# The load of v for batches 4 to 7 is requested behind the first gate block of the next group

## The chip, the cores and the metric

The kernel runs on one core of one Trainium2 chip. The metric is the device time of one execution in microseconds (us), the median of the runs. The engines are named as in the profile: PE (matrix products; PEld is its weight load), DVE, ACT, POOL, and SP, which only issues transfers. POOL issues all loads of q, k and v, so its instruction order also sets the order of these transfers.

## The reference

The computation has two parts, one after the other. The first is attention with a sliding window and a decay per head, for 8 batches of 8 heads, 576 rows and 64 columns. The second is a feed-forward block on the 4608 x 512 result.

```python
scores = scale * np.matmul(q, k.transpose(0, 1, 3, 2))      # 8 batches, 8 heads, 576 x 576
mask = (rel >= 0) & (rel < 128)
scores = np.where(mask, scores + bias[None], -1e9)
attn = softmax(scores)
x = np.matmul(attn, v)                                       # then reshaped to (4608, 512)
g, val = x @ w_gate, x @ w_val                               # (512, 1536) each
out = (gelu(g) * val) @ w_out                                # (1536, 512)
```

## The kernel before

All order is written by hand: each engine executes its instructions in the order of the program, and nothing is moved by a scheduler.

The feed-forward block goes over 9 groups of 512 tokens (`g` = 0 to 8), attention over 8 batches of 576 rows. They are interleaved: while group `g` is in its feed-forward block, the batch `b = g + 2` is in its scores and the batch `b - 1 = g + 1` in its values. A group has two stretches.

* **The gate stretch**, twelve blocks `f` = 0 to 11 of 128 hidden columns. For blocks 0 to 5 and 10 and 11, `gate_val` (L659) makes the products with `w_gate` and `w_val`; ACT takes gelu of the one (L666) and DVE multiplies it with the other into `hT` (L667). Blocks 6 to 9 go together through `gate_quad` (L842), which needs seven products on sums of x instead of eight. POOL makes these sums (`combine_x`, L800), and POOL multiplies the upper halves of the quad's hidden values (L889).
* **The output stretch**, `out_products` (L762): the product with `w_out`, also seven products instead of eight, called `P(1)` to `P(7)`, each for two halves `a` = 0 and 1. They need sums of hidden blocks, `combine_left` (L737); POOL makes those of blocks 0 to 5, DVE those of blocks 6 to 11 at f = 11, behind POOL's L889. Between the products stand the scores of batch g + 2 (`scores2`, L307; exponentials on ACT, L236; masks on DVE, L241) and the values of batch g + 1 (`values`, L508), which read `vb`. Results leave PSUM through `gather_out` (L909 to L924); where a product adds on to a PSUM bank (`P(4)` after `P(7)`, say), the bank has to be read first, for `P(4, 0)` by DVE's L919.

Transfers. POOL requests q, k and v of a batch with five DMA instructions each (`load`, L117: four of 128 rows and one of 64). q and k go to the tiles `qs` and `ks`; SP turns them into `qT` and `kT` with transposing transfers at the start of the next group (`transposes_dma`, L180 and L187), behind the landing of q and k. v goes straight to `vb[b % 2]`, where the values read it, one group and a half after the request. The tile `vb[g % 2]` also holds the gelu values of group g's quad.

Three places on POOL matter here. At f = 3, a copy of two elements of block 3 into the tile `mark` (L1336) makes POOL wait until DVE has written block 3; behind it stand `combine_x` and four `combine_left`. (In group 2 the same place is f = 0.) At f = 5 two more `combine_left` stand. At f = 6 stands the quad with L889, and right behind it the requests: q and k of batch g + 3, then v of batch g + 2.

Of the kernel before, what the change touches and what calls it, by code (L numbers as in the profile page):

```python
# [36 lines left out]
def kernel(  # L37
# [10 lines left out]
    nc = tc.nc  # L48
    B, H, S, D = q.shape
# [49 lines left out]
    mark = consts.tile([1, 2], BF16, name="mark")  # L99
# [13 lines left out]
    def load(t, src, b, js=range(5), last=0):  # L113
        for j in js:
            n = rows(j)
            at = last if j == 4 else 0
            nc.gpsimd.dma_start(  # L117
                out=t[at:at + n, j, :].rearrange("p (h d) -> p h d", h=H),
                in_=src[b][:, 128 * j:128 * j + n, :].rearrange("h p d -> p h d"))
# [5 lines left out]
    def load_v(b, js=range(5)):  # L125
        load(vb[b % 2], v, b, js, 64)
# [44 lines left out]
    def transpose(b, what, c, copy):  # L171
        ps = bank().bitcast(BF16)
        for n, lo in ((0, 0), (1, 384)):
            transpose_runs(b, n, what, c, ps[:, lo:576])
        for n, lo in ((0, 0), (1, 384)):
            untangle(copy, b, n, what, c, c + 1, ps[:, lo:576])

    def transposes_dma(b):
        def of_k():
            nc.sync.dma_start_transpose(  # L180
                out=kT[b % 2].rearrange("p c (j t) -> p (c j) t", t=128),
                in_=ks[b % 2].rearrange("p j x -> p (j x)"))

        if b > 4:
            of_k()
        for j in range(5):
            nc.sync.dma_start_transpose(  # L187
                out=qT[b % 2][:, :, 128 * j:128 * j + 128], in_=qs[b % 2][:, j, :])
        if b <= 4:
            of_k()  # L190
# [193 lines left out]
    def add(b, c0, copy=None, what=(0, 2, 1)):  # L384
        hs = slice(2 * c0, 2 * c0 + 4)
        P = Ps[b % 2].rearrange("p h (n y) -> p h n y", y=64)[:, hs]
        to = T.rearrange("p h (n y) -> p h n y", y=64)[:, hs]
        if 0 in what:
            for x in (0, 1):
                half = slice(64 * x, 64 * x + 64)  # L390
                nc.vector.tensor_tensor(
                    out=to[half, :, x:x + 7:2], in0=P[half, :, 0:10:3], in1=P[half, :, 1:11:3],
                    op=ALU.add)
        if 2 in what:
            nc.vector.tensor_copy(out=to[0:64, :, 8], in_=P[0:64, :, 12])
            nc.vector.tensor_tensor(
                out=to[64:128, :, 8], in0=P[64:128, :, 11], in1=P[64:128, :, 12], op=ALU.add)
        if 1 in what:
            for x in (0, 1):
                half, n = slice(64 * x, 64 * x + 64), 4 - x  # L400
                (copy or nc.vector.tensor_copy)(
                    out=to[half, :, x + 1:x + 2 * n:2], in_=P[half, :, 2:3 * n:3])
# [237 lines left out]
    hid = {}  # L640
# [43 lines left out]
    def store():  # L684
        for args in stores:
            nc.sync.dma_start(**args)
        stores.clear()
# [41 lines left out]
    def combine_left(g, lo, hi, which=(0, 1, 2, 3), engine=nc.vector):  # L729
        x, ns = halves(g), slice(lo, hi)  # L730
        a11, a12, a21, a22 = (x[:, ns, e, h, :] for h in (0, 1) for e in (0, 1))
        s1, s2, s4 = (left[:, n, ns, :] for n in range(3))
        steps = ((s1, a21, a22, ALU.add), (s2, s1, a11, ALU.subtract),
                 (s4, a12, s2, ALU.subtract), (a21, a11, a21, ALU.subtract))
        for n in which:
            to, a, b, op = steps[n]
            engine.tensor_tensor(out=to, in0=a, in1=b, op=op)  # L737
# [215 lines left out]
    for h in (0, 2, 4, 6):  # L953
        for w, src in ((0, q), (1, k)):
            (nc.scalar if w and h == 0 else nc.sync).dma_start(
                out=raw[w][h // 4].rearrange("p (h x) -> p h x", h=4)[:, h % 4:h % 4 + 2, :],
                in_=src[0][h:h + 2, 0:384, :].rearrange("h (p r) d -> p h (r d)", r=3))
# [114 lines left out]
    for do in inverse_a:  # L1072
        do[1]()
    dve(out=pairs1.rearrange("p x (h d) -> p h x d", d=64),
        in_=vb[1].rearrange("p j x -> p (j x)")[:, 0:1536].rearrange(
            "p (h x d) -> p h x d", h=H, x=3))
# [46 lines left out]
    for n in range(4):  # L1123
        nc.gpsimd.dma_start(
            out=wo[:, 3 * n:3 * n + 3, :],
            in_=moe_w_out[384 * n:384 * n + 384, :].rearrange("(c p) f -> p c f", p=128))
# [155 lines left out]
    for g in range(NG):  # L1282
        if 1 <= g < B - 2:
            transposes_dma(3 if g == 1 else g + 2)
        if g >= B - 1:
            for f in range(NF):
                if f in QUADS:
                    gate_quad(g, f)
                elif not any(f0 < f < f0 + 4 for f0 in QUADS):
                    gate_val(g, f)  # L1290
                if f == 4:
                    store()
                if f == 5:
                    combine_left(g, 0, 2, (0, 1), engine=nc.gpsimd)
                if f == 6:
                    combine_left(g, 2, 3, (0, 1))
                    combine_left(g, 0, 2, (3, 2), engine=nc.gpsimd)
            for which in ((0, 1), (3,), (2,)):
                for lo, hi in ((3, 5), (5, 6)) if 0 in which else ((2, 5), (5, 6)):
                    combine_left(g, lo, hi, which)  # L1300
            out_products(g)
            continue
        if g == 1:
            room = rooms(1)
            sums = combine_weights(6, nc.vector)
            for do in sums[:5]:
                do()
        for f in range(9 if g == 0 else 0, NF):
            if f == 6 and g:
                gate_quad(g, 6, room if g == 1 else None,  # L1310
                          (lambda: gather(g + 1)) if g in (2, B - 2) else None)
            elif not (g and 6 < f < 10):
                gate_val(g, f)
            if g == 1:
                for do in {0: sums[5:7], 1: sums[7:]}.get(f, ()):
                    do()
                if f in (1, 2, 3):
                    combine_x(1, 0, 256, {1: (0,), 2: (1, 2), 3: (3,)}[f])
                if f in (4, 5, 10, 11):
                    combine_right({4: 0, 5: 1, 10: 2, 11: 3}[f])  # L1320
            if f in put_off:
                put_off.pop(f)()
            if f == 1:
                store()
            if g == 0 and f == 10:
                masks_of_last_blocks(0, 8)
            if g == 0 and f == 9:
                for c in range(4):
                    for w in (0, 1):
                        transpose(1, w, c, (act, dve)[w])  # L1330
            if g < 2:
                continue
            if g == 2 and f == 2:
                add(3, 2, act, (1,))
            if f == (0 if g == 2 else 3):
                nc.gpsimd.tensor_copy(out=mark, in_=hid[g][0:1, f, 510:512])  # L1336
                combine_x(g, engine=nc.gpsimd)
            if f == 3 and 2 < g < B - 2:
                combine_left(g, 0, 2, (0, 1, 3, 2), engine=nc.gpsimd)
            if f == (5 if g == 2 else 4):  # L1340
                sums4(g + 1)
            if f == 5:
                if 2 < g < B - 2:
                    combine_left(g, 2, 3, (0, 1), engine=nc.gpsimd)
                    gather(g + 1)
                else:
                    combine_left(g, 0, 3, (0, 1), engine=nc.gpsimd)
            if g == B - 2 and f == 2:
                combine_x(g + 1, 0, 192)
            if f == (11 if g == 2 else 6):  # L1350
                spread_dma(g + 1)
            if f == 6:
                if g + 3 < B:
                    load_qk(g + 3)
                if g + 2 < B:
                    load_v(g + 2)
            if f == 11:
                combine_left(g, 3, 6, (0, 1))
        if g == 1:
            nc.gpsimd.tensor_copy(out=mark, in_=kT[1][0:1, 0, 512:514])  # L1360
            load_qk(4)
            load_v(3)
        if g == 0:
            nc.gpsimd.memset(Ps[0][:, :, 0:64], 0.0)
            for t in (qs[1], ks[1]):
                nc.gpsimd.memset(t[64:128, 4, :], 0.0)
        if g in PRODUCTS:
            out_products(g)
        else:
            for item in steps(g):  # L1370
                if isinstance(item, int):
                    out_part(g, item)
                else:
                    RUN[item[0]](*item[1:])
            store()
        if g == 0:
            load_v(2)
            nc.gpsimd.tensor_copy(out=mark, in_=qT[0][0:1, 0, 512:514])
            load_qk(3)
# [30 lines left out]
```

## Time and profile before

| | |
|---|---|
| runs | 328.99, 327.66, 327.49 us (median 327.66) |
| the profiled execution | 328.3 us, span in the profile 326.5 us |
| busy share of the span | PE 97%, DVE 79%, ACT 67%, POOL 60% |
| granted PE clock | full in all 40 slices |
| groups 3, 4 and 5, from block 0 to the next group's block 0 | 33.77, 33.77 and 33.78 us |

Times in rows are us from the start of the span. A row of the timeline gives start, length, engine, line, operation, tiles and shapes, the number of instructions that were merged, and in brackets how long the engine had been idle and what ended the wait. The length of a merged row runs from its first start to its last end. A row of the windows gives the length of the stretch, then the busy us of each engine with the number of its instructions in parentheses, the granted clock, the DMA share and GB/s.

### The profile page before, as it was taken

Reading aid. Unit: us, or ns where it says so; the run is one execution under the profiler, and the core shown is the slowest. Engines: PE = TensorE matmul, PEld = TensorE weight load, DVE = VectorE, ACT = ScalarE, POOL = GpSimd, SP = SyncE. Lnnn points to the kernel's source line nnn. Section 1 sums busy time; section 2 is a strip of 40 time slices with the busy share of each in tenths; the row PEclk is TensorE's granted clock in tenths of the full one; section 3 lists DMA queues with packets and bytes.
Section 4 is the critical chain, followed back from the end, with each engine's and each line's share of the span. In section 5 each row is a group of like instructions: output and inputs, shape, how many; then the busy total and the mean of one; then the engine's idle time right before and its main releaser. Section 6 shows DMA issues by size and latency. Waiting matters only on the chain.

```text
span 326.5 us, 9488 instructions
## 1 busy us (share of the span) xinstructions
PE 317.4 (97%) x3784; PEld 215.8 (66%) x3784; DVE 256.8 (79%) x506; ACT 219.0 (67%) x417; POOL 195.6 (60%) x224
## 2 busy tenths in 40 slices
PE   8999998999999998999999999999999999999995
PEld 6566645575554767566856685578657787788764
DVE  7889766778779987868798679867996786876692
ACT  8974687567798675857875787578767246636641
POOL 6974689194079897189936994595029475410450
PEclk9999999999999999999999999999999999999999
DMA  8999999999999979976996499949200530003003
GB/s 215 168 196 191 202 173 178 128 160 177 131 175 165 171 147 201 155 137 159 186 190 121 137 182 181 134 126 203 89 15 22 130 130 2 0 2 130 3 0 129
DMA packets 149920, 43.57 MB, mean 133 GB/s; under 512 B 133588, under 2 KB 142964, under 8 KB 149876
## 3 DMA queue, kind: packets, MB, share of 16 engines
q0 software_dynamic: 107456, 18.10, 73.8%
q1 hardware_dynamic: 39104, 18.55, 27.0%
q10 hardware_dynamic: 3316, 6.32, 8.4%
q8 instruction: 29, 0.48, 0.6%
q14 instruction: 15, 0.12, 0.1%
HBM read 43.65 MB, written 9.53 MB: 163 GB/s over the span
## 4 chain that ended last, share of the span: by engine, by line
PE 89%; ACT 3%; DVE 3%; issue 2%; DMA 1%; SPq 0%; ACTq 0%; DVEq 0%
PE ps L659 36%; PE ps L842 18%; PE ps L762 18%; PE ps L508 5%; PE ps L696 4%; ACT P L236 2%; PE ps L307 2%; PE ps L716 2%; PE ps L221 1%; DMA qs<-in_q_dram 1%; PE ps L444 1%; DVE ks L800 1%; PE ps L159 1%; ACT osb L917 1%; DVE xT L547 0%
## 5 line engine op out<-in xcount | busy, mean ns | idle before, releaser
L659 PE MATMUL ps<-xT,wg 128*128 128x512 bf16 (+4 forms) x312 | 71.8, 352 | 0.0
L659 PE MATMUL ps<-xT,wv 128*128 128x512 bf16 (+4 forms) x312 | 71.7, 352 | 0.0
L666 ACT ACTIVATE gelu<-ps 128x512 bf16<-128x512 f32 (+3 forms) x77 | 41.6, 546 | 35.0 <-PE ps L659 31.8
L667 DVE TENSOR_TENSOR hT<-ps,gelu 128x512 bf16<-128x512 f32 (+3 forms) x77 | 46.6, 622 | 19.6 <-PE ps L659 9.4
L236 ACT ACTIVATE P<-ps 128x512 bf16<-128x512 f32 (+1 forms) x108 | 52.3, 577 | 4.1 <-PE ps L307 2.5
L659 PEld LDWEIGHTS <-wv 128*128 128x128 bf16 x312 | 29.5, 98 | 29.7 <-DVE xT L567 0.2
L659 PEld LDWEIGHTS <-wg 128*128 128x128 bf16 x312 | 28.7, 98 | 26.0 <-issue 0.3
L117 POOL DMA_DIRECT2D vb<-in_v_dram x40 | 34.1, 888 | 7.9 <-DMA ks<-in_k_dram 5.9
L241 DVE TENSOR_TENSOR P<-P,emask 128x768 bf16<-128x768 bf16 x60 | 32.0, 553 | 7.3 <-ACT P L236 5.5
L762 PEld LDWEIGHTS <-hT 128*128 128x128 bf16 x336 | 31.9, 97 | 7.6 <-issue 1.0
L887 POOL TENSOR_TENSOR hT<-qT,qs 128x512 bf16<-128x512 f32 x10 | 11.5, 1166 | 30.1 <-ACT qs L853 30.1
L842 PEld LDWEIGHTS <-kept 128*128 128x128 bf16 x256 | 25.0, 98 | 2.9
L762 PEld LDWEIGHTS <-left 128*128 128x128 bf16 x252 | 24.1, 98 | 4.0 <-DVE left L737 0.8
L117 POOL DMA_DIRECT2D ks<-in_k_dram x30 | 25.4, 889 | 1.9 <-DMA qs<-in_q_dram 1.9
L117 POOL DMA_DIRECT2D qs<-in_q_dram x30 | 25.4, 863 | 1.6 <-DMA wo<-in_moe_w_out_dram 0.8
L1336 POOL COPY mark<-hT 1x2 bf16<-1x2 bf16 x5 | 0.9, 174 | 41.3 <-DVE hT L667 41.2
L762 PE MATMUL ps<-right,hT 128*128 128x256 bf16 x168 | 22.2, 272 | 0.6 <-DVE osb L919 0.4
L762 PE MATMUL ps<-right,left 128*128 128x256 bf16 x168 | 20.6, 273 | 0.5 <-DVE left L737 0.5
L762 PE MATMUL ps<-wo,hT 128*128 128x256 bf16 x168 | 21.0, 273 | 0.0
L508 PE MATMUL ps<-P,vb 64*64 64x192 bf16 (+2 forms) x752 | 18.4, 221 | 1.8 <-issue 1.0
L850 DVE TENSOR_TENSOR P<-ps,P 128x512 f32<-128x512 f32 x24 | 15.0, 682 | 6.3 <-PE ps L842 4.3
L850 DVE TENSOR_TENSOR qT<-ps,qT 128x512 f32<-128x512 f32 x20 | 12.9, 686 | 8.9 <-PE ps L842 7.5
(170 smaller groups left out, 624.4 us busy)
## 6 DMA issues: line engine op xcount, KB each, us to landing
out_dram<-osb SPq DMA_DIRECT2D x34, 256.0 KB
rb<-rd ACTq DMA_DIRECT2D x10, 576.0 KB
vb<-in_v_dram POOLq DMA_DIRECT2D x32, 128.0 KB, 6.5
qs<-in_q_dram POOLq DMA_DIRECT2D x24, 128.0 KB, 5.9
ks<-in_k_dram POOLq DMA_DIRECT2D x24, 128.0 KB, 7.7
wo<-in_moe_w_out_dram POOLq DMA_DIRECT2D x4, 384.0 KB, 12.0
wg<-in_moe_w_gate_dram POOLq DMA_DIRECT2D x5, 256.0 KB, 7.2
wv<-in_moe_w_val_dram POOLq DMA_DIRECT2D x5, 256.0 KB, 9.0
```

The source lines that it names most:

```text
L117: nc.gpsimd.dma_start(out=t[at:at + n, j, :].rearrange("p (h d) -> p h d", h=H), in_=src[b][:, 128 * j:128 * j + n, :].rearrange("h p d -> ...
L236: nc.scalar.activation(out=dst, in_=src, func=AF.Exp, scale=0.125)
L241: nc.vector.tensor_tensor(out=dst, in0=dst, in1=m, op=ALU.mult)
L508: mm = nc.tensor.matmul(out=out, lhsT=lhsT, rhs=prob(b)[half, c, i, col:col + q1 - q0], start=all(t[2] != u for t in todo[:n]), stop=True, ...
L659: nc.tensor.matmul(out=ps[:, a:e], lhsT=w[:, c, 128 * f:128 * (f + 1)], rhs=xT[:, c, t0 + lo + a:t0 + lo + e], start=begins and a == 0, st ...
L666: nc.scalar.activation(out=gl[:, 0:n], in_=pg, func=AF.Gelu)
L667: nc.vector.tensor_tensor(out=hid[g][:, f, lo:hi], in0=pv, in1=gl[:, 0:n], op=ALU.mult)
L696: nc.tensor.matmul(out=acc[g], lhsT=hid[g][:, f, 128 * t:128 * (t + 1)], rhs=wo[:, f, :], start=(f == 0), stop=(f == NF - 1))
L762: nc.tensor.matmul(out=made[g, a, into], lhsT=lhsT, rhs=rhs, start=first and i == 0, stop=i == NF // 2 - 1, skip_group_check=True)
L842: nc.tensor.matmul(out=ps[:, 256 * e:256 * e + 256], lhsT=w[:, c, at:at + 128], rhs=x[:, c, :], start=n in (1, 2, 5) and e == 0 and c == 0 ...
L850: nc.vector.tensor_tensor(out=to[u], in0=cut(banks[n, u], to[u].shape[1]), in1=to[u], op=ALU.add)
L887: nc.gpsimd.tensor_tensor(out=out, in0=P5[u], in1=high, op=ALU.mult)
```

## The change

The five requests for v of batch g + 2 behind the quad of group g (g = 2 to 5, batches 4 to 7) are taken out. In groups 3 to 6, behind the gate block f = 0, POOL now copies two elements of that block into `mark`, so that it waits for DVE's write of block 0, and then issues the five requests for v of batch g + 1, which is the batch whose values are made at the end of the same group. The batches 0 to 3, all loads of q and k, and everything on the other engines stay.

```diff
@@ -1332,6 +1332,9 @@
                 continue
             if g == 2 and f == 2:
                 add(3, 2, act, (1,))
+            if g > 2 and f == 0 and g + 1 < B:
+                nc.gpsimd.tensor_copy(out=mark, in_=hid[g][0:1, f, 510:512])
+                load_v(g + 1)
             if f == (0 if g == 2 else 3):
                 nc.gpsimd.tensor_copy(out=mark, in_=hid[g][0:1, f, 510:512])
                 combine_x(g, engine=nc.gpsimd)
@@ -1352,8 +1355,6 @@
             if f == 6:
                 if g + 3 < B:
                     load_qk(g + 3)
-                if g + 2 < B:
-                    load_v(g + 2)
             if f == 11:
                 combine_left(g, 3, 6, (0, 1))
```

The program's instruction order on POOL, between the quad of group 3 and block 3 of group 4 (the name ks_97 is the second k tile, vb_104 the second v tile, here of batch 5; DMASW is a transfer semaphore of POOL's queue):

```order
 L117 DMA ks_97<-in_k_dram 64x8x64 [waits DMASW2_49]
-L117 DMA vb_104<-in_v_dram 128x8x64 [waits DMASW3_49,DVE_49]
-L117 DMA vb_104<-in_v_dram 128x8x64 [waits DMASW4_49,DVE_49]
+L1336 COPY mark<-hT 1x2 [waits DVE_49]
+L117 DMA vb_104<-in_v_dram 128x8x64 [waits DMASW3_49]
+L117 DMA vb_104<-in_v_dram 128x8x64 [waits DMASW4_49]
 L117 DMA vb_104<-in_v_dram 128x8x64 [waits DMASW5_49,Pool_49]
 L117 DMA vb_104<-in_v_dram 128x8x64 [waits DMASW6_49,Pool_49]
 L117 DMA vb_104<-in_v_dram 64x8x64 [waits DMASW7_49]
-L1336 COPY mark<-hT 1x2 [waits DVE_49]
+L1339 COPY mark<-hT 1x2 [waits DVE_49,Pool_49]
 L800 TENSOR_TENSOR left<-xT 128x512 [waits PE_49]
```

Here the new copy stands ahead of the five requests, which so wait for block 0 of group 4; the copy that waits for block 3 (now L1339) and `combine_x` stand directly behind them, as before. One instruction per group is added.

The same engine between the quad of group 5 and block 3 of group 6 (batch 7, for which no q and k follow):

```order
 L889 TENSOR_TENSOR hT<-P_106,vb_104 128x2x256 [waits Activation_49] x2
-L117 DMA vb_104<-in_v_dram 128x8x64 [waits DMASW7_49,DVE_49]
-L117 DMA vb_104<-in_v_dram 128x8x64 [waits DMASW0_49,DVE_49]
+L1336 COPY mark<-hT 1x2 [waits DVE_49]
+L117 DMA vb_104<-in_v_dram 128x8x64 [waits DMASW7_49]
+L117 DMA vb_104<-in_v_dram 128x8x64 [waits DMASW0_49]
 L117 DMA vb_104<-in_v_dram 128x8x64 [waits DMASW1_49,Pool_49]
 L117 DMA vb_104<-in_v_dram 128x8x64 [waits DMASW2_49,Pool_49]
 L117 DMA vb_104<-in_v_dram 64x8x64 [waits DMASW3_49]
-L1336 COPY mark<-hT 1x2 [waits DVE_49]
+L1339 COPY mark<-hT 1x2 [waits DVE_49,Pool_49]
 L800 TENSOR_TENSOR left<-xT 128x512 [waits PE_49]
```

Again only the wait in front of the five requests is new. The rows of PE, DVE, ACT and SP are the same in both programs but for the line numbers of the launch.

## The prediction

> **What bounds the kernel now.** I read the page's chain of work that ended last first (its shares by engine), then windows by group.
>
> ```profile
> PE 89%; ACT 3%; DVE 3%; issue 2%; DMA 1%; SPq 0%; ACTq 0%; DVEq 0%
> 96.38:131.92 35.54, 34.10 (x413) 23.22 (x414) 31.43 (x60) 25.40 (x47) 30.25 (x33) 1.00 1.73 169
> 131.92:165.69 33.77, 33.60 (x413) 23.08 (x412) 26.65 (x54) 24.50 (x43) 25.94 (x29) 1.00 1.37 163
> 165.69:199.46 33.77, 33.60 (x413) 23.08 (x412) 27.70 (x58) 24.51 (x43) 25.25 (x29) 1.00 1.32 160
> 199.46:233.24 33.78, 33.60 (x414) 23.11 (x412) 27.70 (x58) 24.52 (x43) 16.92 (x19) 1.00 1.07 141
> 233.24:265.36 32.12, 31.60 (x323) 21.40 (x322) 26.55 (x54) 17.57 (x30) 17.47 (x17) 1.00 0.25 72
> ```
>
> The windows are groups 2 to 6, the only ones that the change reaches; the first number after the length is PE's busy time. PE sets the end: in groups 3 to 5 it is busy for 33.60 of some 33.77 us. All its idle time in the five groups is 1.44 + 0.17 + 0.17 + 0.18 + 0.52 = 2.48 us. That is all that better transfers could win. No transfer of v stands in the chain. So the question is whether POOL, delayed, makes PE wait.
>
> **The change part by part.** What is taken away first, in group 4, the model for group 5 (the same schedule 33.77 us later):
>
> ```profile
> 161.43 4.27 POOL L117 DMA_DIRECT2D vb<-in_v_dram  x5
> 173.97 0.17 POOL L1336 COPY mark<-hT 1x2 bf16<-1x2 bf16 x1 [8.28 <-DVE hT L667]
> 184.63 2.27 POOL L889 TENSOR_TENSOR hT<-P,vb 128x512 bf16<-128x512 f32 x2
> ```
>
> The five requests are the last things POOL did before it sat idle for 8.28 us until block 3. Their removal frees 4.27 us that nobody waits for: worth 0.
>
> What is put in: the wait for block 0, the small copy, and the same five requests. Block 0's product is the first of the two that DVE makes here:
>
> ```profile
> 169.29 1.29 DVE L667 TENSOR_TENSOR hT<-ps,gelu 128x512 bf16<-128x512 f32 x2
> 172.46 1.45 DVE L667 TENSOR_TENSOR hT<-ps,gelu 128x512 bf16<-128x512 f32 x2
> 186.44 0.69 DVE L667 TENSOR_TENSOR hT<-ps,gelu 128x512 bf16<-128x512 f32 x1 [0.22 <-PE ps L659]
> 187.24 0.56 DVE L737 TENSOR_TENSOR left<-hT 128x768 bf16<-128x768 bf16 x1
> 187.83 0.56 DVE L737 TENSOR_TENSOR left<-left,hT 128x768 bf16<-128x768 bf16 x1
> 190.66 0.42 DVE L919 TENSOR_TENSOR osb<-ps,osb 128x256 f32<-128x256 f32 x1
> 189.00:191.00 2.00, 2.00 (x20) 1.77 (x19) 2.00 (x6) 2.00 (x6) 2.00 (x3) 1.00 1.67 186
> ```
>
> One such product takes 0.69, so block 0 is written at 169.29 + 0.69 = 169.98. I take 0.06 from a DVE write to the copy behind it (an estimate: the second row's products end with block 3 at 172.46 + 1.45 = 173.91, the copy starts at 173.97). Copy at 170.04 to 170.21, five requests to 174.48. The copy for block 3 started at 173.97, so POOL is now late by **0.51 us**. Whether time passes between such a copy and the request behind it, two places show differently (both fives stand directly behind one):
>
> ```profile
> 66.25 4.19 POOL L117 DMA_DIRECT2D qs<-in_q_dram  x5
> 91.90 4.27 POOL L117 DMA_DIRECT2D qs<-in_q_dram  x5 [0.36 <-issue]
> ```
>
> No idle time at the first, 0.36 at the second. I take none, since the requests of the change wait for transfers that were issued over 8 us earlier, and keep 0.51 + 0.36 = 0.87 as the upper bound.
>
> Where does the delay go? From block 3 to L889, POOL has no more than short gaps, so L889 ends not at 186.90 but at 187.41 (bound 187.77). `combine_x` has room:
>
> ```profile
> 175.34 1.15 POOL L800 TENSOR_TENSOR left<-xT,left 128x512 bf16<-128x512 bf16 x1
> 178.35 2.78 PE L842 MATMUL ps<-left,kept 128*128 128x256 bf16 x24
> ```
>
> Its second sum is done at 176.49 and the first product on sums (24 matmuls on `left`) begins at 178.35, 1.9 us later; a later POOL by more than that would stop PE there. But DVE's first L737 reads what L889 writes. It started at 187.24, directly behind DVE's own last product (186.44 + 0.69 = 187.13); now it can start at 187.41 + 0.06 = 187.47. **DVE is late by 0.23 us** (bound 0.59); 0.28 of POOL's delay is free. DVE has no gap up to L919 (2.00 of 2.00 us busy), so L919 moves by as much. And PE waits there: `P(4, 0)` adds to the bank that L919 reads.
>
> ```profile
> 188.38 1.48 PE L762 MATMUL ps<-right,left 128*128 128x256 bf16 x12
> 191.13 0.81 PE L762 MATMUL ps<-right,hT 128*128 128x256 bf16 x6
> 118.63 0.56 DVE L737 TENSOR_TENSOR left<-left,hT 128x768 bf16<-128x768 bf16 x1
> 119.17 1.48 PE L762 MATMUL ps<-right,left 128*128 128x256 bf16 x12
> 121.97 0.42 DVE L919 TENSOR_TENSOR osb<-ps,osb 128x256 f32<-128x256 f32 x1
> 122.44 0.81 PE L762 MATMUL ps<-right,hT 128*128 128x256 bf16 x6 [0.20 <-DVE osb L919]
> ```
>
> L919 ends at 191.08, `P(4, 0)` starts at 191.13. Group 2 shows what a longer DVE does at the same place: from the second L737 to L919 it takes 3.34 us instead of 2.83, and PE takes 3.27 from `P(6, 0)` to `P(4, 0)` instead of 2.75. 0.51 on DVE cost 0.52 on PE: one to one. So group 4 costs 0.23 (at most 0.59), group 5 the same.
>
> Groups 3 and 6 have more room:
>
> ```profile
> 134.38 0.69 DVE L667 TENSOR_TENSOR hT<-ps,gelu 128x512 bf16<-128x512 f32 x1
> 140.20 0.17 POOL L1336 COPY mark<-hT 1x2 bf16<-1x2 bf16 x1 [6.98 <-DVE hT L667]
> 236.84 1.29 DVE L667 TENSOR_TENSOR hT<-ps,gelu 128x512 bf16<-128x512 f32 x2
> 242.56 0.17 POOL L1336 COPY mark<-hT 1x2 bf16<-1x2 bf16 x1 [17.68 <-DVE hT L667]
> ```
>
> With 0.06 + 0.17 + 4.27 = 4.50 behind block 0, the run of requests ends at 135.07 + 4.50 = 139.57 in group 3 and 237.53 + 4.50 = 242.03 in group 6; both are 0.5 to 0.6 before the copy for block 3. They cost 0; without that cover, each 0.1 that the run lasts longer delays POOL by 0.1.
>
> The transfers themselves: v now moves while SP's transposes do.
>
> ```profile
> 170.84 7.21 SPq L187 DMA_TRANSPOSE qT<-qs  x5
> 72.53 8.67 SPq L187 DMA_TRANSPOSE qT<-qs  x5
> 187.58 0.87 PE L307 MATMUL ps<-qT,kT 64*64 64x64 bf16 x44
> vb<-in_v_dram POOLq DMA_DIRECT2D x32, 128.0 KB, 6.5
> 196.08 0.67 PE L508 MATMUL ps<-P,vb 64*64 64x192 bf16 x26
> ```
>
> Beside loads of q and k, at 72.53, the five transposes took 8.67 instead of 7.21 us. 1.5 us more puts the last issue at 179.6 instead of 178.1, and PE reads them at 187.58: hidden by some 8 us; a delay beyond that would reach PE one to one. v lands 6.5 us after its request, near 181, and is read at 196.08: 15 us to spare.
>
> One more thing may stretch the run of requests: DVE's small copies in the same stretch (L395, put off to block 1).
>
> ```profile
> 98.35 0.48 DVE L395 COPY T<-P 64x256 bf16<-64x256 bf16 x1
> L395 DVE COPY T<-P x10: 211/218/481, 98.4 to 239.5; 64x256 bf16<-64x256 bf16 x10
> ```
>
> Of ten such copies one took 481 ns instead of 218, in the midst of POOL's requests for k. If POOL is held as long as one undisturbed copy lasts, the run is 0.22 longer; the fives of requests that I read, with DVE 75 to 99% busy beside them, all took 4.19 to 4.28, so I take 0 and keep 0.22 as a bound.
>
> [...]
>
> Sum: 2 x 0.23 = **+0.46 us**, bounds 0 and 2 x (0.59 + 0.22) = 1.62. The profiled execution took 328.3 (span 326.5 and 1.8 around it); 328.3 + 0.46 = 328.76. The median of the runs is 0.64 lower, so I say **328.1**.
>
> **The rivals.**
>
> *Hidden altogether* (327.7). If DVE is not gapless, or L889 ends earlier than its rough span says, 0.23 us vanishes. For it: spans on POOL are rough, and the term is small. Against it: group 2's one-to-one.
>
> *Relief on the queue* (327.2). PE stands once for want of instructions while POOL's loads are in flight:
>
> ```profile
> 127.22 2.65 POOL L117 DMA_DIRECT2D vb<-in_v_dram  x3
> 129.33 0.95 issue
> ```
>
> In group 2, v of batch 4 was being requested at the time of this stall. If less traffic ends that stall, 0.95 is won and 0.46 paid. Against it: q and k had been requested first and remain. To be faster by over 0.5%, 2.1 of all 2.48 idle us would have to go.
>
> *POOL's run of requests decides* (329.3, slower). One mechanism: the run between block 0 and block 3 on POOL gets longer, through the 0.36 gap and the 0.22 hold, L889 comes late, and DVE's L737 hands it to PE. Each group of 4 and 5 costs the delay less 0.28: from a delay of 1.10 each, the loss exceeds 1.64 us; at 0.51 + 0.36 + 0.22 = 1.09 it is 1.62. Beyond, groups 3 and 6 use up their half microsecond and begin to pay as well. For it: 0.36 was seen once, and the copy of 0.48. Against: no five requests took over 4.28.
>
> **How the numbers follow.** Forecast (0 to 1.2 us more, 327.7 to 328.8) 0.50; hidden 0.25; relief 0.12, a third of it beyond 0.5%; POOL's run 0.13, counted as slower by over 0.5%. Half a per cent, 1.64 us, is about what a measurement can tell from no change. So: faster 0.04, same 0.83, slower 0.13. Range: from relief without any cost, 327.66 - 0.95 = 326.7, to 329.3.
>
> **What would show it.** The five requests stand behind the copy at about 170.2 and end at 174.5; POOL's copy for block 3 is late by half a microsecond in groups 4 and 5 and on time in 3 and 6; L737 on DVE starts 0.2 later behind L889; group 4's window is some 34.0 long, with the loss at `P(4, 0)`. I am wrong if a row of requests is much longer than 4.3 us, if SP's transposes last beyond 185, if groups 3 or 6 change too, or if the 0.95 us stall goes or comes elsewhere.

## The result, and the profile after

The changed kernel is slower, and by more than was forecast. Median of 7 runs 330.27 us (329.46 to 331.18), against 328.76 us (327.49 to 328.99) of 7 runs of the kernel before in the same comparison: a ratio of 1.006, 95% interval 1.0035 to 1.0086, so 1.2 to 2.8 us. The forecast was 328.1, the range ended at 329.3. The profiled execution of the changed kernel took 331.0 us (span 329.2).

The shares of its chain of waits first. After that the windows of groups 3, 4 and 5, from block 0 to the next group's block 0.

```profile
PE 82%; DMA 7%; ACT 3%; DVE 3%; issue 2%; SPq 1%; ACTq 0%; POOL 0%; DVEq 0%
133.57:168.14 34.57, 33.79 (x410) 23.05 (x412) 26.23 (x50) 23.89 (x43) 25.45 (x29) 0.99 1.29 156
168.14:202.06 33.92, 33.47 (x410) 23.07 (x412) 27.70 (x58) 24.51 (x43) 25.39 (x29) 1.00 1.38 159
202.06:235.98 33.92, 33.47 (x410) 23.08 (x412) 27.68 (x57) 24.51 (x43) 17.02 (x19) 1.00 0.81 124
```

Groups 4 and 5 grew by 0.15 us each, from 33.77 to 33.92: the term that was forecast is there, a little smaller. But group 3, which was to cost nothing, grew by 0.80, and the chain now holds 7% of transfers where it had 1%. More than half of these 7% lie far ahead of the change, in a load of w_out (12.41 us from 33.27 on); what is new in the changed groups is one transfer in group 3. First the chain's rows there, then two waits of PE:

```profile
138.41 7.28 DMA qT<-qs
145.69 0.02 issue
145.71 0.02 ACTq L457
145.73 0.04 issue
145.77 0.53 ACTq L457
146.30 0.04 issue
146.34 0.59 ACT P L860
146.93 0.05 issue
```

```profile
PE ps L508 <- issue: 1.8, 1, 1.8
...
PE ps L842 <- ACT P L860: 0.3, 1, 0.3
```

Read the chain from the bottom: PE's quad (L842) waits for ACT's copy L860, which empties its bank; ACT makes that copy behind L457, a transfer that ACT itself issues; and L457 waits until SP's transposing transfer of q has landed, 7.28 us after its issue. No tile connects the two: L457 (`gather`) brings the row sums of the softmax (`sumrow` to `rd`), the transpose brings q. What connects them is a semaphore. The program's order on SP and ACT in group 3 (DMAHW with a number is the semaphore of a transfer from these two queues; the program has eight of them and gives them out in turn):

```
SP   L180 DMA_TRANSPOSE kT_102<-ks_98 128x20x128 [waits ... DMAHW0_49 ...]
SP   L187 DMA_TRANSPOSE qT_100<-qs_96 128x4x128 [waits DMAHW1_49]
SP   L187 DMA_TRANSPOSE qT_100<-qs_96 128x4x128 [waits DMAHW2_49]
ACT  L457 DMA rd<-r 2x8x128 [waits DMAHW0_49,DVE_49]
ACT  L457 DMA rd<-r 2x8x160 [waits DMAHW1_49,DVE_49]
ACT  L860 COPY P_106<-ps 128x2x256 [waits PE_49] x2
```

By its row each of these transfers waits on its own semaphore, until the one before it there has landed; ACT's second gather then starts 0.08 us behind the landing of q's transpose (below). ACT's two gathers have numbers 0 and 1, and so stand behind k's transpose and the first one of q. That is so in both kernels. Now the timeline of ACT at this place, the kernel before and the changed one:

```profile
142.25 1.54 ACTq L457 DMA_DIRECT2D rd<-r  x2
143.83 1.07 ACT L860 COPY P<-ps 128x512 f32<-128x512 f32 x2 [1.06 <-DVE hT L667]
```

```profile
144.14 2.16 ACTq L457 DMA_DIRECT2D rd<-r  x2
146.34 1.07 ACT L860 COPY P<-ps 128x512 f32<-128x512 f32 x2 [1.68 <-PE ps L842]
146.98 1.19 PE L842 MATMUL ps<-left,kept 128*128 128x256 bf16 x9 [0.34 <-ACT P L860]
```

Before, the first q transpose was issued at 138.47 and its semaphore complete at 141.77, after 3.30 us; the second gather came at 143.26 and found it so. After, it was issued at 138.41 and complete at 145.69; the second gather started at 145.77, 0.08 behind. (Landings are read from the trace's semaphore counts, here and below.) The bracket of L860 names PE's quad, but L860 began 1.62 us behind the quad's first product (144.72), where 1.00 was enough before (142.83 and 143.83); it began 0.04 behind the gather in both. v is what came in between: on POOL's timeline its five requests for group 3 begin 1.8 us ahead of that transpose.

```profile
136.63 4.18 POOL L117 DMA_DIRECT2D vb<-in_v_dram  x5
142.16 0.17 POOL L1339 COPY mark<-hT 1x2 bf16<-1x2 bf16 x1 [1.34 <-DVE hT L667]
```

In group 4 they begin at 172.75, 0.3 us behind the first q transpose (172.45), which then lands after 3.48 us, well ahead of the gathers at 178.46. So only group 3 has this wait.

The rest of the profiled pair can't be put down to the change. The shift of the same weight load on PE, after less before, goes: -0.5 up to group 2's last stretch (mostly a stall near 55 us, 0.93 us idle, that only this profile of the kernel before has), +0.8 at the stall L508 of group 2 (1.77 us instead of 0.95), +1.5 directly behind it, +0.6 at the quad of group 3, +0.15 and +0.16 in groups 4 and 5; together 2.7, as 331.0 stands to 328.3. The profile calls the stall "issue": nothing that it shows was waited for. That PE waits there for instructions, as the prediction has it, is not shown: a packet of 16 KB on the queue of instructions took from 128.20 to 129.16, but the stall goes on to 130.63. The length of the stall L508 does not follow the change: it was 0.9 to 1.1 us in ten of the twelve profiles, with v of batch 4 moved or not, 1.77 in this one, and 1.70 in one where that v was not moved. The +1.5 is the clock, in windows of 2 us:

```profile
129.00:131.00 2.00, 0.37 (x3) 0.26 (x3) 2.00 (x7) 0.00 (x0) 0.00 (x0) 0.88 1.74 239
131.00:133.00 2.00, 2.00 (x11) 1.43 (x10) 1.19 (x6) 0.66 (x2) 0.00 (x0) 0.50 2.35 150
133.00:135.00 2.00, 1.95 (x9) 0.99 (x9) 1.40 (x4) 1.29 (x2) 0.00 (x0) 0.77 0.49 37
```

The granted clock is at half for 3.4 us at the end of the stall and behind it, and the products go at little more than half the pace: six of L762 (`right`, `hT`) take 1.46 us at 130.82, and 0.83 at the same place of the kernel before. The end of the half clock, 0.2 us of the loss, lies in group 3's window. This is not what makes the kernel slower: of its 7 runs, four had a full clock throughout, and they took 329.61, 330.16, 330.27 and 331.18.

### The profile page after: what moved, and what is told of

Read it like the earlier page. It is cut to its first block, busy times and chain, and to the rows that moved or that the text cites. A ratio compares the mean times of both kernels' runs of the same rounds, so it can differ in the third digit from the quotient of the medians.

```text
span 329.2 us, 9457 instructions
## 1 busy us (share of the span) xinstructions
PE 316.6 (96%) x3753; PEld 216.3 (66%) x3784; DVE 256.2 (78%) x506; ACT 218.5 (66%) x417; POOL 196.1 (60%) x228
## 4 chain that ended last, share of the span: by engine, by line
PE 82%; DMA 7%; ACT 3%; DVE 3%; issue 2%; SPq 1%; ACTq 0%; POOL 0%; DVEq 0%
PE ps L659 31%; PE ps L762 18%; PE ps L842 18%; PE ps L508 5%; PE ps L696 4%; DMA wo<-in_moe_w_out_dram 4%; PE ps L307 2%; DMA qT<-qs 2%; ACT P L236 2%; DMA qs<-in_q_dram 1%; PE ps L221 1%; PE ps L444 1%; DVE ks L800 1%; PE ps L716 1%; SPq L180 1%
## 5 line engine op out<-in xcount | busy, mean ns | idle before, releaser
L659 PE MATMUL ps<-xT,wg 128*128 128x512 bf16 (+4 forms) x294 | 69.5, 351 | 1.5 <-issue 0.6
L762 PEld LDWEIGHTS <-hT 128*128 128x128 bf16 x336 | 32.2, 98 | 8.1 <-issue 1.4
L842 PEld LDWEIGHTS <-kept 128*128 128x128 bf16 x256 | 25.0, 98 | 3.5 <-ACT P L860 0.6
L762 PEld LDWEIGHTS <-left 128*128 128x128 bf16 x252 | 24.4, 99 | 4.3 <-DVE left L737 0.8
L762 PE MATMUL ps<-right,hT 128*128 128x256 bf16 x168 | 22.8, 277 | 0.8 <-DVE osb L919 0.7
L762 PE MATMUL ps<-right,left 128*128 128x256 bf16 x168 | 20.6, 273 | 0.5 <-DVE left L737 0.5
L762 PE MATMUL ps<-wo,hT 128*128 128x256 bf16 x168 | 21.0, 273 | 0.0
L508 PE MATMUL ps<-P,vb 64*64 64x192 bf16 (+2 forms) x752 | 18.3, 221 | 2.6 <-issue 1.8
```

Source lines behind the costliest of these rows:

```text
L508: mm = nc.tensor.matmul(out=out, lhsT=lhsT, rhs=prob(b)[half, c, i, col:col + q1 - q0], start=all(t[2] != u for t in todo[:n]), stop=True, ...
L659: nc.tensor.matmul(out=ps[:, a:e], lhsT=w[:, c, 128 * f:128 * (f + 1)], rhs=xT[:, c, t0 + lo + a:t0 + lo + e], start=begins and a == 0, st ...
L762: nc.tensor.matmul(out=made[g, a, into], lhsT=lhsT, rhs=rhs, start=first and i == 0, stop=i == NF // 2 - 1, skip_group_check=True)
L842: nc.tensor.matmul(out=ps[:, 256 * e:256 * e + 256], lhsT=w[:, c, at:at + 128], rhs=x[:, c, :], start=n in (1, 2, 5) and e == 0 and c == 0 ...
```

## The experiments

The theory: a transfer of v that is requested just ahead of SP's transposes makes the first of these land late; ACT's gather shares its semaphore and waits; the quad of group 3 waits for ACT. It adds to the forecast's term for POOL in groups 4 and 5. The rivals: POOL's lateness makes the whole loss (the prediction's last rival); or the loss is chance, from the stalls and the clock, which no part of the change sets.

### The two kernels again, unchanged

Both programs once more, without an edit.

> The kernel before, unchanged, for a second profile and more times. If the stall for instructions on PE in group 2 and the lower clock behind it are drawn by chance in both kernels (theory A), some runs of this kernel show a granted clock under 1.000 or a stall of more than 1.5 us there too, and its times spread over 1.3 us or more. If the change causes them (theory B), every clock here is 1.000 and the stall stays near 0.95 us. Groups 3, 4 and 5 take 33.77 us each in both cases, to 0.03.

> The changed kernel, unchanged, for a second profile and more times. Own theory (POOL late, DVE's sums behind it): groups 4 and 5 take 33.92 us each (+0.15) again, group 6 as before. Lane theory (ACT's gather of the sums waits for a transposing transfer that v has delayed): in group 3 PE waits again about 0.6 us at the quad's first product on sums, beside that group 3 takes 33.77 us. If group 3's wait came only with the low clock that preceded it in the first profile, it is absent where the clock is 1.000.

The kernel before: 328.65 us in 12 runs, against 328.41 in 29 runs of the comparison (1.0004, 0.9983 to 1.0025). The changed one: 330.16 in 12 runs (1.0048, 1.0021 to 1.0076), so +1.6 us, as in the result. Its profiled execution had the clock full in every slice (mean 1.000), a stall at L508 of 1.04, and the wait at the quad none the less. Its chain in group 3, then its PE:

```profile
137.08 6.88 DMA qT<-qs
...
144.04 0.53 ACTq L457
144.57 0.04 issue
144.61 0.59 ACT P L860
```

```profile
145.25 1.95 PE L842 MATMUL ps<-left,kept 128*128 128x256 bf16 x16 [0.77 <-ACT P L860]
```

The first product on sums of the quad comes 1.04 us later than in the kernel before, against the product ahead of it, and 0.98 of it stays; groups 4 and 5 lose 0.18 and 0.16. So the wait recurs, it needs no halved clock, and chance does not make the loss. In the result's pair it was 0.6 because PE itself had just lost 1.5 us to the clock and came later to the quad.

The profile of the kernel before shows what chance does. It lost 1.44 us in group 2, at the quad, since POOL's own requests there waited for earlier transfers (rows of POOL, then of PE):

```profile
103.39 1.76 POOL L117 DMA_DIRECT2D vb<-in_v_dram  x2 [1.21 <-DMA qs<-in_q_dram]
...
107.86 1.14 POOL L800 TENSOR_TENSOR left<-xT 128x512 bf16<-128x512 bf16 x1
```

```profile
110.29 1.91 PE L842 MATMUL ps<-left,kept 128*128 128x256 bf16 x16 [1.27 <-POOL left L800]
```

This wait stands ahead of the first changed instruction. Single runs of the one unchanged program lay between 327.62 and 330.62.

### POOL late, v left where it was

The kernel before, with work for POOL alone in place of the requests:

```diff
+            if g > 2 and f == 0 and g + 1 < B:
+                nc.gpsimd.tensor_copy(out=mark, in_=hid[g][0:1, f, 510:512])
+                for _ in range(15):
+                    nc.gpsimd.memset(scratch, 0.0)
```

`scratch` is a new tile that nothing reads.

> The kernel before, with POOL alone delayed: behind block 0 of groups 3 to 6 the same copy and then 15 small memsets (about 4.2 us) on a scratch tile; v stays where it was, so no transfer moves. Own theory: groups 4 and 5 take 33.92 us each (+0.15), 3 and 6 are unchanged, in all +0.3 us. If the moved transfers are what costs (lane theory, or contention), groups 3 to 6 are as in the kernel before and the time is the same within 0.1 us; the rest of the +1.9 us between the means is then not POOL's.

331.24 us in 6 runs (1.0085, 1.0058 to 1.0112). The dose was larger than meant:

```profile
170.30 0.18 POOL L1337 COPY mark<-hT 1x2 bf16<-1x2 bf16 x1 [4.02 <-DVE hT L668]
170.42 5.54 POOL L1339 MEMSET scratch<- 128x256 bf16 x15
175.91 0.18 POOL L1341 COPY mark<-hT 1x2 bf16<-1x2 bf16 x1
```

From the first copy to the copy for block 3 it is 5.61 us, where the kernel before would have 3.93 (the distance of the two blocks on DVE): POOL is late by 1.68. Groups 4 and 5 lost 1.36 each for it, group 3 lost 0.14, group 6 nothing: 2.86 in all, and the medians differ by 2.83. In the changed kernel the same distance is 4.39, with the copies at:

```profile
172.50 0.18 POOL L1336 COPY mark<-hT 1x2 bf16<-1x2 bf16 x1 [9.02 <-DVE hT L667]
172.75 4.20 POOL L117 DMA_DIRECT2D vb<-in_v_dram  x5
176.89 0.17 POOL L1339 COPY mark<-hT 1x2 bf16<-1x2 bf16 x1
```

So it is late by 0.46 there, and loses 0.15 to 0.18. Two doses, 0.46 and 1.68, cost 0.15 and 1.36: on both, all but some 0.31 us of the delay reaches PE. That confirms the forecast's path from POOL by way of DVE to PE, one to one beyond the free part, and shows that this path at the dose of the change makes 0.3 us in all, not 1.6. The rival that POOL makes the whole loss falls.

### The q transposes ahead of k's, for batch 5

The changed kernel, with SP's order in group 3 turned round, so that the gathers share their semaphores with the first two transposes of q, which now go out first:

```diff
-        if b > 4:
+        if b > 5:
             of_k()
...
-        if b <= 4:
+        if b <= 5:
             of_k()
```

The same edit of the kernel before is the control.

> The changed kernel with one order turned in group 3: the five transposes of q are issued before that of k, so that the two gathers of the sums share their transfer semaphores with the first two transposes of q, which are issued some 4 us earlier, and not with k's and the first of q. Lane theory: PE's wait of 0.6 us at the quad of group 3 is gone, ACT's two gathers take 1.5 us together, as before the change, and not 2.2. If it is plain contention on the queues, the gathers still take over 2 us and the wait stays. Groups 4 and 5 stay at 33.92.

> The kernel before with the transposes of q ahead of that of k in group 3, the control for the same turn in the changed kernel. Semaphore theory: there was no wait to remove, groups 3 to 5 stay at 33.77 us and the time is that of the kernel before within 0.3 us. If the turn is a gain of its own (some 1.5 us, which would mean that the wait in group 3 was not what it took away), this kernel is that much faster than the kernel before.

The changed kernel with this edit: 328.41 us in 12 runs, the same as the kernel before in that comparison (1.0003, 0.9985 to 1.0021), and 1.75 below the changed kernel beside it. The control: 328.19 us in 12 runs (0.9993, 0.9969 to 1.0017), so the edit is worth nothing by itself that could be measured. The wait is gone, on SP, ACT and PE:

```profile
128.69 7.75 SPq L187 DMA_TRANSPOSE qT<-qs  x5
136.68 4.62 SPq L180 DMA_TRANSPOSE kT<-ks  x1
```

```profile
142.05 1.54 ACTq L457 DMA_DIRECT2D rd<-r  x2
```

```profile
144.39 2.78 PE L842 MATMUL ps<-left,kept 128*128 128x256 bf16 x24
```

The two transposes now go out at 128.69 and 130.00 and have landed by 136.90, 5.1 us ahead of the first gather (142.05). They too were slow, 7.86 and 6.90 us, beside the loads of k (in the changed kernel the last of these was requested at 126.97 and landed at 135.12); what is gone is the gather that came too soon for them. k's transpose, last, lands 10.4 us after its issue and holds up no gather. v is requested as in the changed kernel. Groups 4 and 5 still lost 0.15 and 0.17. Together with the reverse test below it decides: in group 3, v's transfer costs only through the transfer that ACT's gather stands behind.

### The wait moved to another transpose

The reverse test. One of SP's stores in group 3 goes out in two halves, which takes one more semaphore, so that the gathers now share theirs with the first and the second q transpose:

```diff
+            if f == 1 and g == 3:
+                args = stores.pop(0)
+                for cols in (slice(0, 256), slice(256, 512)):
+                    nc.sync.dma_start(out=args["out"][:, cols], in_=args["in_"][:, cols])
```

> The changed kernel with one store in group 3 split into two halves, so that one transfer more stands between the transposes and ACT's gathers, and the gathers share their semaphores with the first and the second transpose of q, no longer with k's and the first. Semaphore theory: the second gather now starts when the second transpose of q has landed, 1.3 us later than in the changed kernel (by its second profile: 145.28 against 143.97), ACT's gathers take 3.5 to 3.9 us and PE's wait at the quad grows from about 0.8 to about 2.1 us. If the gathers are slow because the queues are full, one more store changes nothing at the quad beyond 0.2 us.

332.52 us in 9 runs (1.0106, 1.0071 to 1.0142). The program's rows:

```
ACT  L457 DMA rd<-r 2x8x128 [waits DMAHW1_49,DVE_49]
ACT  L457 DMA rd<-r 2x8x160 [waits DMAHW2_49,DVE_49]
```

The chain of the profile, and PE at the quad:

```profile
139.15 7.15 DMA qT<-qs
...
146.38 0.53 ACTq L457
```

```profile
147.59 0.82 PE L842 MATMUL ps<-left,kept 128*128 128x256 bf16 x3 [2.29 <-ACT P L860]
```

The second gather follows the second transpose (complete at 146.31) by 0.07 us, as it followed the first one before, and the quad's first product on sums comes 2.55 us late. So here the transfer that is waited for went with the number of the semaphore: one more store, which has nothing to do with q, moved the wait from q's first transpose to its second. Behind this wait the clock was at half for 3.4 us, some 1.7 us more in this execution (an estimate, half of the 3.4).

### v of batch 4 alone, and of batches 5 to 7 alone

The changed kernel with only group 3's request moved, and with only those of groups 4 to 6 moved (`g + 1 in (4,)` and `g + 1 in (5, 6, 7)` as the condition).

> Only v of batch 4 is moved (requested in group 3 behind block 0); v of batches 5 to 7 stays behind the quads. Semaphore theory: ACT's second gather in group 3 waits for the first transpose of q again, PE loses 0.6 to 1.1 us at the quad of group 3; groups 4 and 5 are back at 33.77 us; the time lies 0.8 to 1.5 us above the kernel before. If the loss came from all four moves alike, only about a quarter of it is here, 0.4 us.

> Only v of batches 5 to 7 is moved; v of batch 4 stays behind the quad of group 2. Own theory: POOL is late in groups 4 and 5 by about half a microsecond, they take 33.90 to 33.92 us, group 3 33.77; the time lies 0.3 us above the kernel before. If the four moves cost alike, it lies 1.3 us above.

Batch 4 alone: 329.60 us in 12 runs against 328.17 (1.0025, 1.0000 to 1.0050). Its profile has the wait of group 3 (the first q transpose lands after 7.33 us, the second gather starts 0.08 later), a shift of 1.44 us there, of which 1.38 stays, and none in groups 4 and 5:

```profile
145.83 1.41 PE L842 MATMUL ps<-left,kept 128*128 128x256 bf16 x11 [1.18 <-ACT P L860]
```

Batches 5 to 7 alone: 329.27 us in 12 runs (1.0026, 0.9998 to 1.0054). Its profile has no wait in group 3 and a loss of 0.18 and 0.17 in groups 4 and 5. The profiles part the change as the theory says. The times do not: 0.35 of loss in the profile should not come out as +1.1 in the medians, and what this profile lost beyond it lay ahead of the first changed place, 3.1 us in group 2 and before. With half an interval of 0.8 to 0.9 us, the times of these two runs can't size the parts, nor rule out that the moves cost alike; only the profiles do that.

### The wait of group 2

Since waits of POOL in group 2 might be what spreads the runs, the load of v for batch 3 was split there, with its last two requests behind `combine_x` of group 2: in the kernel before, and in the changed kernel with the q transposes first.

```diff
+                if g == 2:
+                    load_v(3, (3, 4))
...
-            load_v(3)
+            load_v(3, (0, 1, 2))
```

> An attempt at a version that beats both: the kernel before, but of the five requests for v of batch 3 only three stay behind q and k of batch 4 (end of group 1); the last two stand in group 2 behind combine_x, so that their wait for earlier transfers no longer holds up the sums that the quad of group 2 needs. In two of the four profiles of kernels that are the same up to there, PE waited 1.3 to 1.4 us for these sums (POOL, L800) at that quad, in the others 0. If that wait is what spreads the times of the kernel before, it is 0 here, the slow end of the times (329.2 to 331.4) thins out, and the median is 0.3 to 0.7 us lower, which the timing may not resolve. If POOL's two requests behind combine_x make its part of the quad (L889) late, as in groups 4 and 5, up to 0.3 us of it goes again.

> The same split of batch 3's requests on the changed kernel with q's transposes first in group 3. Expected: no wait at the quads of groups 2 and 3, groups 4 and 5 at 33.92 us; 0.3 us above the split kernel before, and 1.8 to 2.2 us under the changed kernel.

The kernel before so edited: 328.26 us in 12 runs (1.0003, 0.9983 to 1.0022). No gain. Its profile has no wait at the quad of group 2, and another one instead, for k's transpose:

```profile
PE ps L307 <- DMA kT<-ks: 2.5, 2, 1.4
```

The changed kernel so edited: 328.53 us in 12 runs (1.0020, 1.0001 to 1.0038), 0.27 above the split kernel before, about as expected, and no better than the kernel before. Its profile has no wait at the quads of groups 2 and 3, and 0.16 and 0.17 of loss in groups 4 and 5. No version of these beats the kernel before.

## Why the prediction was wrong

**What bounds the kernel** was read rightly: PE sets the end, and what counts is whether it is made to wait.

**The requests taken out, worth 0**: right. Nothing was won behind the quads, and the stall that the relief rival would have ended is still there: 1.8 and 1.0 us in the two profiles of the changed kernel, 0.95 before.

**POOL late in groups 4 and 5**: right in its path but for the last bank, and a little large. Forecast were 4.44 us from copy to copy and 0.51 of delay; measured 4.39 and 0.46. Forecast were 0.28 free and 0.23 lost; measured 0.31 and 0.15 to 0.18. First the rows of DVE and PE behind L889 in group 4 of the changed kernel, then two of the kernel before:

```profile
189.84 0.56 DVE L737 TENSOR_TENSOR left<-hT 128x768 bf16<-128x768 bf16 x1 [0.26 <-POOL hT L889]
190.83 1.48 PE L762 MATMUL ps<-right,left 128*128 128x256 bf16 x12
191.85 0.42 DVE L911 COPY osb<-ps 128x256 f32<-128x256 f32 x1
192.32 0.81 PE L762 MATMUL ps<-right,hT 128*128 128x256 bf16 x6
```

```profile
189.25 0.43 DVE L911 COPY osb<-ps 128x256 f32<-128x256 f32 x1
189.73 0.82 PE L762 MATMUL ps<-right,hT 128*128 128x256 bf16 x6
```

L737 starts 21.70 us into the group instead of 21.55. PE loses its 0.14 between its two rows, 1.49 us instead of 1.35. The second of them is `P(7, 0)`. It adds on to the bank that DVE's L911 reads, and it starts 0.05 behind the end of L911 in both kernels (192.27 and 189.68). So DVE's 0.15 reaches PE at a bank that has to be read first, as the prediction had it, but one bank earlier: at `P(7, 0)` through L911, and not at `P(4, 0)` through L919. With the larger dose most of the loss comes earlier still, at the products that read what L737 writes (L738 there):

```profile
190.07 1.16 PE L763 MATMUL ps<-right,left 128*128 128x256 bf16 x9 [0.94 <-DVE left L738]
```

The upper bounds did not come into play: the runs of five requests in groups 3 to 5 took 4.18 to 4.20, with no gap shown in front. Of DVE's small copies beside them one took 0.44 us (139.74, group 3), twice the median of 0.22, and those of groups 4 and 5 took 0.22. POOL's five requests beside the long one took 4.18 us, no longer than the others. So no run shows the hold of 0.22 that the upper bound has for POOL beside such a copy.

**Groups 3 and 6 cost 0**: right for POOL (in group 3 it stood idle for 1.34 us ahead of the copy for block 3), wrong for group 3 as a whole.

**The step that failed** is the one on the transfers themselves: "1.5 us more puts the last issue at 179.6 instead of 178.1, and PE reads them at 187.58: hidden by some 8 us". Two things in it were wrong. The delay was priced by how long SP takes to issue, and that hardly changed (the five q transposes of group 3 took 6.97 us before and 7.48 after), while the landing of the first went from 3.30 to 7.28 us. And the only readers considered were those of the data. In its place the runs show a second reader, of the semaphore: ACT's second gather. It was ready at 143.26, 1.01 behind the first one (142.25) and 1.49 behind the landing at 141.77; 1.49 was all the room there was, not 8. Where it must wait, PE loses what the gather is late against that 1.01, one to one: 0.62 late and 0.61 lost at the quad's first product on sums in the result's profile, 1.05 and 1.04 in the changed kernel again, 1.46 and 1.44 with batch 4 alone, 2.56 and 2.55 with the split store (where the first gather waited too, and is counted from when it could have started, 142.81). The step also argued from group 4 as a model. There SP's transposes start 0.98 us into the group and block 0's product 3.60; in group 3 it is 2.35 and 2.46 (kernel before). So v goes out behind the first transpose of q in the one and ahead of it in the other.

In all four profiles where the gather waited, it started 0.07 to 0.08 us after the transpose's semaphore was complete (145.77, 144.04, 144.62 and 146.38, against 145.69, 143.97, 144.54 and 146.31).

**The sum.** Of the 2.2 us between the 328.1 of the forecast and 330.27, 1.1 is its base: the median of the kernel before was 327.66 in three runs and 328.76 in the seven of the comparison. As a difference, 0.46 was forecast. The upper bound of 1.62 would have held the 1.5 that the medians differ by, but by luck: it was made of POOL's gap and hold, which did not come. Profiles give 0.55 to 1.4 for group 3 and 0.3 for groups 4 and 5, together 0.9 to 1.7; the medians give +1.5 and +1.75 against the kernel before and against the version that takes the wait away. What stays open is how much of the medians' difference is more than this: in the profiles, stalls and waits in group 2 differ by 1 to 2 us between executions, the two of the unchanged kernel among them, and whether the change alters how often they come can't be told from one profile of each.

**The chances.** Slower by over half a per cent had 0.13, all of it for POOL's run of requests. None of the three rivals was what happened; a rival for waits that ACT meets on its own queue was missing.

## What to carry to other kernels

In this program, which gives eight semaphores out in turn, a transfer had more readers than those of its tile: the next transfer on the same semaphore waited for it (ACT's second gather, started 0.07 to 0.08 us behind the landing of a transpose that SP had issued) and held up what stood behind it on its engine (ACT's L860, started 0.04 us behind the gather). Where a program gives semaphores out like this and a load is moved, list for every queue which transfers are in flight together and which semaphore each has, and give every landing that gets later its room up to the next issue on that semaphore, group by group. Price the lateness by landings, not by how long the issuing engine is busy: here the issues of the five transposes went from 6.97 to 7.48 us, the landing of the first from 3.30 to 7.28.

## What the hardware showed unexpectedly

* **Landing beside v.** A transpose of 128 rows of q landed 3.30 us after its issue when POOL's last load had landed 0.36 us before it (138.11), and 6.9 to 7.3 us after it in four profiles where v's requests began 1.6 to 2.1 us earlier (7.28, 6.88, 7.33, 6.94). It is not only v: issued among loads of k, with q first in the changed kernel, it took 7.86.
* **Half the clock behind two waits of PE.** Behind the stall of 1.77 us (changed kernel) and behind 2.29 us of waiting at the quad (the split store) the granted clock was 0.5 for 3.4 us. Behind 1.70 us (the split load of v) it stayed at 1.00, and so it did behind 0.8 to 1.4 us elsewhere. The windows of the split store where it shows:

```profile
146.00:148.00 2.00, 0.41 (x3) 0.29 (x4) 0.43 (x1) 1.05 (x2) 1.92 (x3) 0.91 1.22 324
148.00:150.00 2.00, 2.00 (x11) 1.44 (x10) 0.86 (x2) 1.09 (x3) 2.00 (x2) 0.50 0.24 80
```

  In these two executions the wait so cost nearly twice itself: 1.77 us and 1.5 more, 2.29 us and 1.7 more (the estimate above).
* **Memory sets on POOL.** Fifteen of 128 x 256 took 5.54 us, 0.37 each.
